# Local attention and a token/channel mixer in one kernel: q and k turned by transfer transposes into a permuted key layout, global query rows scored apart, part of the ReLUs on VectorE

## The chip, the cores and the metric

The kernel runs on one core of one Trainium2 chip. The metric is the device time of one execution in microseconds (us), the time of the slowest core, which here is the only one. A run more than 1.5% above the fastest of its kernel is marked slow. A time of the text is the median of all timed runs; a profile is one execution of them. A ratio is the mean time of one kernel's fast runs over that of the other's of the same rounds, so it is not quite the ratio of the two medians.

Names: PE is TensorE (matmuls), PEld its weight loads, ACT is ScalarE, DVE is VectorE, Pool is GpSimd, SP is SyncE. SP here only issues transfers, in program order.

## The reference

Eight batches, eight heads, 576 positions, head size 64. Attention with a window of 32 positions to each side and eight global positions (which see all and are seen by all), then a mixer: a token MLP (576 to 256 to 576) and a channel MLP (512 to 1536 to 512), each with a residual.

```python
scores = scale * q @ k.T                              # per batch and head
mask = (abs(i - j) <= 32) | is_global[i] | is_global[j]
x = softmax(where(mask, scores, -1e9)) @ v            # heads joined: (8, 576, 512)
h = relu(x.T @ w_tok1) @ w_tok2
u = x + h.T
out = u + relu(u @ w_ch1) @ w_ch2
```

## The kernel before

Per batch the kernel casts q and k to f16, turns them on PE so that the head dimension lies on the partitions (T), lets DVE copy the result out of PSUM (TE), scores five key tiles per pair of heads (S_), takes the exps on ACT and multiplies them by a band mask on DVE (SM). GK and OG handle the global rows and columns, PV multiplies by v, M1 and M2 are the token MLP, M3 turns u by four DMA transposes (uT), M4 is the up-projection (its PSUM tile is b1p) and M5 the down-projection (op). The scheduling is by hand: iteration b merges the "dense" list of batch b (M4, M5) with the "sparse" list of batch b+1 (everything from scores to uT) into one program order, by weights.

```python
def load_v16(b):                       # v of batch b, cast by the transfer, key order as in memory
    for c in range(NT):                # 5 transfers, issued by Pool
        nc.gpsimd.dma_start(out=vsh[b % 2][r0:r1, c, :, 0:D], in_=v[b, :, j0 : j0 + (r1 - r0), :]...)

def T(b, p):                           # 10 transposes on PE per pair of heads
    for ti, n in enumerate((qn, kn)):
        for t in range(NT):
            nc.tensor.transpose(out=pT[:, ti, P*t : P*t+P], in_=n[b % 2][:, t, 2*p : 2*p+2, :], identity=ident)

def TE(b, p):                          # four DVE copies out of PSUM, which also undo the order of the load
    nc.vector.tensor_copy(out=qT..., in_=pm)   # 128x512 f16
    ...

def S_(b, p, part):
    def score(ps, off, c):             # PSUM written without stride; 208 or 144 columns (16 of them global rows)
        for par in range(2):
            nc.tensor.matmul(ps[:, par, off : off + n], lhsT=kT[r, P*c : P*c+P], rhs=qf[r, lo : lo+n], ...)
    ...                                # then 3 exps per pair on ACT

def M3(b, part):                       # u turned by transfer
    nc.sync.dma_start_transpose(out=s["uT"][:, :, P*tau : P*tau+P], in_=s["u16"][:, tau, :])

def M4(b, j):
    ...                                # 4 matmuls into b1p
    nc.scalar.activation(out=s["b1"][:, j, :], in_=ps, func=AF.Relu)

# sparse(b), cut:
if b == 1:   u += [(5.0, lambda: None), gather_t(0), ..., t(0), t(1)]   # b1p of batch 0 go first
u += [sa(0), sb(0), t(2), t(3), ..., GK(b), OG(b), PV, M1, load_v16(n), M2, M3, T and TE of batch n]

# start: q,k of batch 0, then v of batch 0 (5 transfers), then q,k of batch 1, all on SP
```

The softmax here doesn't subtract the row's maximum and nothing guards it: scores larger than these inputs give would overflow.

## Time and profile before

| | before |
|---|---|
| time | 357.12 us median (354.12 to 358.76, 4 runs) |
| span of the profiled run | 352.9 us, mean granted PE clock 0.999 |
| first b1p of batch 0 (end of the "start") | 44.3 us |
| seven iterations | 42.6, 42.5, 37.2, 41.0, 36.7, 40.6, 37.1 us |
| tail | 31.0 us |

The table is read from the first b1p matmul of each batch in the timeline, and an iteration runs from one such matmul to the next. Odd iterations are longer because the last 64 rows of two batches are projected together there.

It leaves out the ReLUs: in the stretch that the prediction names, from 207.2 us to the last exp at 219.9, ACT is busy 10.70 of 12.70 us, and waits for b1p for the rest:

```profile
ACT b L611 <- PE b1p L608: 2.0, 3, 0.8
```

### The profile page before, as it was taken

How to read it: one execution, taken by the hardware profiler on the slowest of the kernel's cores; microseconds unless marked ns; L12 is line 12 of the kernel's file. 1: busy time of each engine (PE TensorE's matmuls, PEld its weight loads, DVE VectorE, ACT ScalarE, POOL GpSimd, SP SyncE). 2: the span in 40 equal slices, each digit the busy share in tenths (PEclk: the TensorE clock that was granted, in tenths of full speed). 3: DMA queues.
4: the chain of work that ended last, by engine and by line, in shares of the span. 5: the costliest groups of instructions: out<-in, count | busy, mean ns of one | idle time of the engine just before them, and what ended most of it. 6: DMA issues, size and time to landing. Idle time of an engine off the chain costs nothing.

```text
span 352.9 us, 6771 instructions
## 1 busy us (share of the span) xinstructions
PE 313.1 (89%) x2753; PEld 167.7 (48%) x2753; DVE 205.2 (58%) x450; ACT 172.1 (49%) x308; POOL 67.0 (19%) x106
## 2 busy tenths in 40 slices
PE   0567888897979999999999998999999998998994
PEld 0345444454446454554466453555465453543641
DVE  3998658647654468457654567547754567451021
ACT  2448358721866238650875239642864258212600
POOL 8988836220003000120003000220000000000000
PEclk9999999999999999999999999999999999999999
DMA  6999999595817558387919467485800430024012
GB/s 138 264 276 207 245 225 160 34 115 119 250 37 70 88 125 263 24 76 106 298 34 86 74 154 230 28 102 137 265 3 30 106 76 2 2 74 119 2 59 89
DMA packets 90046, 42.28 MB, mean 120 GB/s; under 512 B 64928, under 2 KB 85280, under 8 KB 90016
## 3 DMA queue, kind: packets, MB, share of 16 engines
q1 hardware_dynamic: 52528, 33.69, 35.9%
q0 software_dynamic: 37200, 8.16, 25.3%
q8 instruction: 21, 0.34, 0.4%
q14 instruction: 9, 0.07, 0.1%
q10 hardware_dynamic: 288, 0.01, 0.0%
HBM read 36.12 MB, written 9.44 MB: 129 GB/s over the span
## 4 chain that ended last, share of the span: by engine, by line
PE 60%; DVE 17%; ACT 13%; DMA 5%; issue 3%; SPq 1%; DVEq 0%; ACTq 0%
PE op L634 23%; PE b1p L608 11%; PE a1p L538 5%; PE hp L562 4%; ACT b L611 4%; DVE e_all L453 3%; ACT e_all L431 3%; PE pv L493 3%; PE pT L393 3%; DMA uT<-u 3%; PE b1lp L621 3%; PE pv L502 3%; ACT e_all L440 2%; PE pv L507 2%; DVE kT L405 2%
## 5 line engine op out<-in xcount | busy, mean ns | idle before, releaser
L608 PE MATMUL b1p<-uT,wc 128*128 128x512 f16 x384 | 94.9, 380 | 4.2 <-DMA uT<-u 4.1
L634 PE MATMUL op<-wc,b 128*128 128x512 f16 x384 | 90.8, 379 | 0.0
L611 ACT ACTIVATE b<-b1p 128x512 f16<-128x512 f32 x96 | 58.4, 625 | 46.1 <-PE b1p L608 45.5
L342 POOL DMA_DIRECT2D vsh<-in_v_dram x35 | 29.6, 850 | 153.8 <-PE pv L507 145.1
L431 ACT ACTIVATE e_all<-s 128x832 f16<-128x832 f32 x32 | 28.5, 892 | 57.1 <-issue 50.7
L634 PEld LDWEIGHTS <-b 128*128 128x128 f16 x384 | 36.2, 98 | 40.1
L608 PEld LDWEIGHTS <-wc 128*128 128x128 f16 x384 | 32.6, 97 | 40.8 <-issue 6.7
L638 DVE TENSOR_TENSOR osb<-u,op 128x512 f32<-128x512 f16 x32 | 22.0, 687 | 44.0 <-PE op L634 43.7
L453 DVE TENSOR_TENSOR e_all<-e_all,bandm 128x1040 f16<-128x1040 f16 x64 | 42.0, 697 | 1.2
L403 DVE COPY qT<-pT 128x512 f16<-128x512 f16 x32 | 22.0, 688 | 17.8 <-PE pT L393 15.7
L522 DVE RECIPROCAL rr<-pv 128x8 f32<-128x8 f32 (+1 forms) x40 | 8.3, 207 | 36.9 <-PE pv L507 28.1
L420 PE MATMUL s<-qT,kT 64*128 64x208 f16 (+1 forms) x320 | 24.7, 254 | 5.6 <-ACT e_all L443 2.3
L523 DVE TENSOR_TENSOR x<-pv,rr 128x512 f16<-128x512 f32 (+1 forms) x40 | 27.6, 691 | 1.4
L502 PE MATMUL pv<-vsh,e_all 128*128 128x66 f16 x320 | 28.3, 197 | 0.0
L502 PEld LDWEIGHTS <-e_all 128*128 128x128 f16 x320 | 24.6, 100 | 4.3 <-issue 2.6
L493 PE MATMUL pv<-rf,lf 128*128 128x264 f16 x80 | 21.6, 284 | 4.0 <-DVE rf L480 2.3
L507 PE MATMUL pv<-vsh,e_all 128*128 128x66 f16 x256 | 24.1, 197 | 0.0
L546 ACT ACTIVATE a<-a1p 128x1024 f16<-128x1024 f32 x7 | 7.2, 1024 | 34.5 <-PE a1p L538 27.4
L420 PEld LDWEIGHTS <-kT 64*128 64x128 f16 x320 | 11.3, 97 | 26.4 <-issue 20.6
L440 ACT ACTIVATE e_all<-s 128x576 f16<-128x576 f32 x32 | 21.9, 684 | 2.8 <-PE s L420 2.8
L567 DVE TENSOR_TENSOR u<-x,hp 128x1024 f16<-128x1024 f16 x14 | 16.9, 1220 | 10.3 <-PE hp L562 10.3
L393 PE MATMUL pT<-ident,qn 128*128 128x128 f16 x160 | 15.3, 230 | 8.1 <-ACT qn L354 4.3
(149 smaller groups left out, 394.6 us busy)
## 6 DMA issues: line engine op xcount, KB each, us to landing
out_dram<-osb SPq DMA_DIRECT2D x32, 256.0 KB, 2.2
lq<-in_q_dram SPq DMA_DIRECT2D x7, 1024.0 KB, 7.1
lk<-in_k_dram SPq DMA_DIRECT2D x7, 1024.0 KB, 8.8
wc<-in_moe_w_ch_dram POOLq DMA_DIRECT2D x6, 512.0 KB, 10.7
vsh<-in_v_dram POOLq DMA_DIRECT2D x21, 128.0 KB, 5.0
vsh<-in_v_dram POOLq DMA_DIRECT2D x14, 96.0 KB, 3.3
lq<-in_q_dram SPq DMA_DIRECT2D x4, 256.0 KB, 5.6
lk<-in_k_dram SPq DMA_DIRECT2D x4, 256.0 KB, 6.2
```

The lines of the kernel that those rows point to most:

```text
L342: nc.gpsimd.dma_start(out=vsh[b % 2][r0:r1, c, :, 0:D], in_=v[b, :, j0 : j0 + (r1 - r0), :].rearrange("h p d -> p h d"),)
L420: nc.tensor.matmul(ps[:, par, off : off + n], lhsT=kT[r, P * c : P * c + P], rhs=qf[r, lo : lo + n], start=True, stop=True,)
L431: nc.scalar.activation(out=e2[:, :, 1:3, 64:EW], in_=ps[:, :, 0 : 2 * W].rearrange("p h (c x) -> p h c x", c=2), func=AF.Exp, scale=scale)
L440: nc.scalar.activation(out=ends, in_=ps[:, :, 0 : 2 * QS].rearrange("p h (c x) -> p h c x", c=2), func=AF.Exp, scale=scale)
L453: nc.vector.tensor_mul(out=eh, in0=eh, in1=bandm)
L493: nc.tensor.matmul(ps[:, hf, 0 : NP * VW], lhsT=s["lf"][:, P * tau - sh : P * tau - sh + P], rhs=s["rf"][:, 2 * hf : 2 * hf + 2], start=b ...
L502: nc.tensor.matmul(o, lhsT=e_all[:, h, tau, EW - P - sh : EW - sh], rhs=vsh[b % 2][:, tau, h, :], start=b == 0 and hh == 0, stop=last and ...
L507: nc.tensor.matmul(o, lhsT=e_all[:, h, tau + 1, 0:P], rhs=vsh[b % 2][:, tau + 1, h, :], start=False, stop=last)
L523: nc.vector.tensor_tensor(out=x16s[b % 2][r, tau, :].rearrange("p (f h x) -> p f h x", f=2, h=NP), in0=pq[r, :, :, 0:D], in1=rr[r].unsquee ...
L608: nc.tensor.matmul(ps, lhsT=wc1[:, cc, P * j : P * j + P], rhs=s["uT"][:, cc, :], start=(cc == 0), stop=(cc == 3))
L611: nc.scalar.activation(out=s["b1"][:, j, :], in_=ps, func=AF.Relu)
L634: nc.tensor.matmul(ps, lhsT=w, rhs=wc2[:, j, :], start=(j == 0), stop=(j == NJ - 1))
```

## The change

The intent is to take work off PE, DVE and ACT. For batches 1 to 7, q and k are turned by DMA transposes out of f16 copies, so 40 PE transposes and their DVE copies per batch vanish. The load puts row 4p+i on partition p, and the transfer leaves keys ordered by i first. Keys are therefore left permuted inside each tile: v must be loaded in the same order, which takes 20 transfers in place of 5. Queries are put back in order by writing the scores into PSUM at a stride of four words. Global query rows leave the scores (192 columns for 208) and are scored apart in GK. Four of the twelve ReLUs per batch go to DVE.

The core of the diff, with cuts marked by dots:

```diff
 def load_v16(b):
-    for c in range(NT):                                     # 5 transfers
+    for rows, c, src in v_parts(b):                         # 20 transfers: 4 residues x 5 tiles
+        nc.gpsimd.dma_start(out=vsh[b % 2][rows, c, :, 0:D], in_=src)
...
+def turn_k(b, c):
+    src = xk[32 * c : 32 * c + 32] if c < NT - 1 else xr[0:32]
+    nc.sync.dma_start_transpose(out=kTs[b % 2][:, c]..., in_=src...)
+def turn_q(b, hp): ...                                      # 8 turns per batch, all on SP
...
 def score(ps, off, c):
-    ps[:, par, off : off + n], lhsT=kT[r, P * c : P * c + P], rhs=qf[r, lo : lo + n]
+    ps[:, par, off : off + n].rearrange("k (x i) -> k i x", i=4), lhsT=kT[r, c, p], rhs=qT[r, p, :, lo:hi]
...
 def GK(b):
+    for c in range(NT):
+        for p in range(NP):                                 # 20 matmuls of 16 columns
+            nc.tensor.matmul(gq[:, c, p], lhsT=kT[:, c, p], rhs=qgz[:, b, p], start=True, stop=True)
+    ...                                                     # then exp (ACT) and a multiply (DVE) into eg, which OG reads
...
+        if j % 2 and j < 8:
+            nc.vector.tensor_scalar(out=s["b1"][:, j, :], in0=ps, scalar1=0.0, scalar2=None, op0=ALU.max)
...
+def qk_pads1():
+    nc.gpsimd.memset(lr[0:32], 0.0)                         # lr takes the last rows of q and k
...
 # start, cut
+    qk_pads1()
     load_rest(1)
     load_qk(1, slice(0, H))
...
 # sparse(b): no dummy ahead of the scores of batch 1 any more; per batch n = b + 1
-    ..., T(n, 0), TE(n, 0), T(n, 1), TE(n, 1)
+    ..., turns of k and q between PV and M1, turn(tq[2]) as the last just ahead of load_v16(n), M2 and M3 (uT)
```

## The prediction

> **What bounds it now.** The page's busy table has PE at 313 of 352.9 us. The first b1p matmul of each batch stands in the timeline at 44.3, 86.8, 129.3, 166.5, 207.5, 244.3, 284.8 and 321.9: a 44 us start, seven iterations (37 us even, 41 us odd from the third on), a 31 us tail. In these iterations PE's gaps are small. With start-to-start times of the trace (512 columns 216 ns, 128-column transpose 56 ns) an even iteration has about 33.1 us of PE work in 36.75. The rest is lost mostly in the scores while ACT runs continuously (207.2 to 220.5, exps and ReLUs).
>
> **Removed per batch.** 40 PE transposes: 2.3 us of PE. Their DVE evictions (4 x (688+180+680+180) ns = 6.9 us) and four eg multiplies (1.0 us). Four of twelve 0.6 us ReLUs leave ACT for DVE (0.69 us each).
>
> **Added per batch.** Twenty 16-column matmuls for global rows: estimated 0.6 us PE, from the 30 ns spacing of the 66-column pv matmuls. They put a chain gk, exp, multiply, og on PE's path, about 1 us. Scores now write PSUM with a stride of four words. The Trainium skill's "PSUM — Partial Sum Buffer" (Specifications) says a non-contiguous pattern slows matmuls significantly; nothing in this trace shows it. At half rate scores cost 1.5 us more, mostly hidden behind ACT. Eight transfer transposes of 9.5 uT-sizes together: SP spends 1.25 us issuing one uT, so an estimated 11 us more of the in-order SP queue, while the engines need only about 0.6 us per uT. ACT gets 12 casts for 10. v takes 20 Pool issues for 5, with slack.
>
> **Steady state.** The ACT-bound part before the global scores shortens from 13.1 to about 11.2 us, so the up-projection phase gains 1.2 us, and transposes at the iteration's end give another 1.2. But the last q turn (about 2.1 us of SP) stands just ahead of the uT transposes in SP's order, and the PE work hiding them shrinks from about 8 to 6.7 us: I expect 2 to 2.7 us of waiting for uT per even iteration, 1 to 1.5 per odd one. Net: even about 36.3, odd 39.5. The first two gain more (42.6 and 42.5 to about 38 and 41).
>
> **Start.** v of batch 0 comes in 20 transfers behind SP's queue, so Pool's casts end near 24.5 rather than 20. Then Pool issues weights and gathers, and only then clears lr; the rest load of k for batch 1 waits for that clear, and the q and k loads behind it on SP. They move from 17 to about 39 us, landing near 50. ACT casts them before the first token ReLU, and scores of batch 1, which need the turns, stand before the first b1p. I expect that b1p at about 60, not 44.3: a loss of about 16 us, which eats the steady gain.
>
> **Sum.** 60+38+41+36.3+39.5+36.3+39.5+36+31 = 357.6 us in the profile, before 352.9; timed runs lie about 1% above. I say 357 us, range 345 to 371. Faster by over 2%: 0.22; within: 0.47; slower: 0.31.
>
> **Would show it.** First b1p near 60 with SP waiting on Pool (right). Waits of b1p for uT around 2 us each in even iterations. Score pairs of 192 columns spaced near 80 ns (no stride cost) or 160. DVE below 170 us busy.
>
> **Could be wrong.** Turns issuing faster or slower than uT by size; a larger stride cost; loads landing sooner; transfers contending so that uT lands late.

## More of the kernel before

The kernel before was run again beside every set of experiments, and its medians lie between 356.4 and 358.6 us.

From the page of the kernel before: the busy table, four rows of the table of 40 slices (busy tenths; PEclk is the granted clock in tenths), and two lines of the table of transfer queues (packets, MB, share of the 16 transfer engines).

```profile
PE 313.1 (89%) x2753; PEld 167.7 (48%) x2753; DVE 205.2 (58%) x450; ACT 172.1 (49%) x308; POOL 67.0 (19%) x106
PE   0567888897979999999999998999999998998994
PEclk9999999999999999999999999999999999999999
DMA  6999999595817558387919467485800430024012
q1 hardware_dynamic: 52528, 33.69, 35.9%
q0 software_dynamic: 37200, 8.16, 25.3%
```

PE is busy through nearly the whole span at full clock, and the transfer engines have slack from the second quarter on. The waits of PE (what it waited for: us in total, times, longest):

```profile
PE b1p L608 <- DMA uT<-u: 4.1, 4, 2.0
PE s L420 <- ACT e_all L443: 2.3, 6, 0.6
PE og L475 <- DVE eg L447: 1.2, 1, 1.2
```

These are small. The groups of instructions by shape (busy us, mean ns | idle before, and what ended it), for the scores on PE and for two of the three exps that read them:

```profile
L420 PE MATMUL s<-qT,kT 64*128 64x208 f16 x192 | 20.7, 267 | 0.8 <-DVE qT L381 0.3 <-DVE kT L409 0.3 <-ACT e_all L431 0.2
L420 PE MATMUL s<-qT,kT 64*128 64x144 f16 x128 | 10.1, 235 | 4.8 <-ACT e_all L443 2.3 <-DVE kT L409 1.3 <-ACT e_all L431 1.0
L431 ACT ACTIVATE e_all<-s 128x832 f16<-128x832 f32 x32 | 28.5, 892 | 57.1 <-issue 50.7 <-PE s L420 6.4
L440 ACT ACTIVATE e_all<-s 128x576 f16<-128x576 f32 x32 | 21.9, 684 | 2.8 <-PE s L420 2.8
```

The exps hardly wait for the scores (6.4 and 2.8 us in the whole run, most of it in the start). This is the reading on which the prediction called that phase bound by ACT.

## The result, and the profile after

The changed kernel took 407.94 us median (405.76 to 409.92, 4 runs) beside 357.12 us (354.12 to 358.76, 4 runs). The ratio of the fast runs is 1.1436, 95% interval 1.1349 to 1.1524: slower by 14%, far outside the predicted range. All outputs are right.

| | before | after | difference |
|---|---|---|---|
| first b1p | 44.27 | 74.69 | +30.4 |
| first iteration | 42.56 | 47.03 | +4.5 |
| next six iterations | 235.1 | 250.9 | +15.8 |
| tail | 31.0 | 31.4 | +0.4 |
| span | 352.9 | 404.0 | +51.1 |

The same parts of the page after:

```profile
PE 320.7 (79%) x2633; PEld 158.3 (39%) x2633; DVE 177.9 (44%) x350; ACT 167.2 (41%) x290; POOL 122.8 (30%) x206
PE   0576013778969999789969998989698999898995
PEclk9979556696998999999989999999989999999999
DMA  7859999991897449974997199929990373003112
q1 hardware_dynamic: 81673, 42.42, 49.6%
q0 software_dynamic: 42464, 8.18, 24.5%
```

DVE and ACT have less to do, as meant, but PE has more, with 120 instructions fewer. The row PE has a hole in the fifth to seventh slice (40 to 70 us), and the granted clock is about half there. Queue q1, which carries the turns, has 29,000 packets more. The waits of PE (hp is the second product of the token MLP, s the scores, og the product of the global rows), and the one of SP that stands behind the start:

```profile
PE hp L639 <- ACT a L604: 22.4, 1, 22.4
PE b1p L669 <- DMA uT<-u: 15.7, 6, 3.9
PE s L473 <- DMA qT<-xq: 8.6, 1, 8.6
PE og L536 <- DVE eg L524: 8.0, 7, 1.2
```

```profile
SPq L137 <- POOL qT L185: 16.2, 1, 16.2
```

Four things in five lines: a long wait in the start, uT late in six iterations, one wait for the first turns, and the chain of the global rows in each iteration. The scores and their exps by shape:

```profile
L473 PE MATMUL s<-qT,kT 64*128 64x192 f16 x256 | 33.7, 392 | 0.1
L473 PE MATMUL s<-qT,kT 64*128 64x128 f16 x64 | 9.5, 293 | 9.1 <-DMA qT<-xq 8.6 <-ACT e_all L490 0.5
L484 ACT ACTIVATE e_all<-s 128x256 f16<-128x256 f32 x32 | 12.3, 384 | 82.2 <-PE s L473 80.9 <-ACT b L675 0.8 <-ACT e_all L490 0.6
```

A matmul of 192 columns has 392 ns where one of 208 had 267. In start-to-start times of the trace, two matmuls of 192 columns (one per half of the array) take 162 ns; before, two of 208 took about 100. The 80.9 us of ACT need care: 68.7 us of it are ACT's pauses ahead of the first exp of batches 1 to 7 (8.2 to 10.7 us each), and the kernel before has that pause too (the 50.7 us under "issue"). Added up gap by gap in the trace, inside the score phases of batches 1 to 7 ACT waits 6.8 us for the scores, where it waited 0.5 before.

The start, from the chain that ended last (start us, us, what). First the kernel before, which has nothing but its own work there, then the changed kernel:

```profile
38.82 0.61 ACT a L543
43.64 0.59 ACT uT L588
44.27 1.89 PE b1p L608 x8
```

```profile
34.47 1.63 POOL wc L268 x2
36.10 1.81 POOL lr L184
37.91 0.26 POOL qT L185
38.82 15.69 DMA lk<-in_k_dram
54.53 2.18 ACT xk L395 x4
58.79 0.50 ACT a L604
62.04 11.55 DMA qT<-xq
74.76 1.82 PE b1p L669 x4
```

Pool clears lr only after its casts of v, the weights and the gathers; q and k of batch 1 stand behind that clear on SP (the view of SP's wait names qT L185, the instruction that follows the clear and starts as it ends); their landing takes 15.7 us; ACT casts them before the first token ReLU (a), for which PE waits 22.4 us; then the last turns of q take 11.6 us to land, and the scores that need them stand ahead of the first b1p. Two stages of the changed kernel by windows (start:end, length, busy times with counts, then granted clock, share of the transfer engines, GB/s):

```profile
50.00:60.00 10.00, 0.67 (x2) 0.25 (x2) 0.00 (x0) 4.75 (x9) 5.99 (x11) 0.50 1.29 133
80.00:90.00 10.00, 7.22 (x63) 3.36 (x62) 6.41 (x16) 5.56 (x10) 4.70 (x8) 1.00 1.25 140
```

PE's clock is halved while it stands idle, and it stays so for a while after: the b1p matmuls that start from 74.7 to 75.5 us are 402 to 427 ns apart, those of a group from 77.1 us on 216 to 226. The Trainium skill's "TensorE: Matmul & The Clock Gate" (Part 1) says that PE goes to half clock after an idle window of about 3.4 us; the trace agrees that a long idle stretch (22.4 us here) halves it. The runs give no sharp length: b1p ran at half rate after a wait of 2.2 us in e3, and at full rate after one of 3.3 us in e12.

The late uT, from the timeline of SP in the iteration that ends at 206.84 us (start us, us, what):

```profile
195.35 1.30 SPq L416 DMA_TRANSPOSE qT<-xq  x1
197.37 1.55 SPq L416 DMA_TRANSPOSE qT<-xq  x1
199.01 5.93 SPq L658 DMA_TRANSPOSE uT<-u  x4
```

and the queues between 200 and 204 us (packets, MB, share):

```profile
q0 software_dynamic: 1665, 0.18, 99.9%
q1 hardware_dynamic: 1612, 0.40, 81.1%
```

u was ready at about 197.8 us. Its four transposes stand behind a turn of q on SP, and they share the transfer engines with the v packets of the next batch (q0), which Pool issued from 191.6 to 201.3 us. Once v is through, q1 alone moved 1830 packets in the 2.5 us from 204.5, against 1612 in the 4 us before.

### The profile page after: what moved, and what is told of

The parts are those of the page before. It is cut to its first block, busy times and chain, and to the rows that moved or that the text cites. A ratio compares the mean times of both kernels' runs of the same rounds, so it can differ in the third digit from the quotient of the medians.

```text
span 404.0 us, 6676 instructions
## 1 busy us (share of the span) xinstructions
PE 320.7 (79%) x2633; PEld 158.3 (39%) x2633; DVE 177.9 (44%) x350; ACT 167.2 (41%) x290; POOL 122.8 (30%) x206
## 4 chain that ended last, share of the span: by engine, by line
PE 63%; DMA 15%; DVE 8%; SPq 5%; POOL 3%; issue 2%; ACT 2%; DVEq 0%; POOLq 0%
PE b1p L669 21%; PE op L698 18%; PE s L473 6%; DMA uT<-u 4%; DMA lk<-in_k_dram 4%; PE a1p L599 4%; PE hp L623 3%; SPq L658 3%; DMA qT<-xq 3%; DMA lv<-in_v_dram 2%; DVE x L584 2%; PE pv L554 2%; PE b1lp L685 2%; PE pv L563 2%; PE pv L568 2%
## 5 line engine op out<-in xcount | busy, mean ns | idle before, releaser
L383 POOL DMA_DIRECT2D vsh<-in_v_dram x140 | 84.1, 622 | 153.8 <-PE pv L568 114.8
L669 PE MATMUL b1p<-uT,wc 128*128 128x512 f16 x384 | 99.2, 398 | 15.7 <-DMA uT<-u 15.7
L675 ACT ACTIVATE b<-b1p 128x512 f16<-128x512 f32 x64 | 38.4, 600 | 62.6 <-PE b1p L669 46.0
L673 DVE TENSOR_SCALAR b<-b1p 128x512 f16<-128x512 f32 x32 | 22.1, 691 | 68.8 <-PE b1p L669 68.8
L490 ACT ACTIVATE e_all<-s 128x768 f16<-128x768 f32 x64 | 50.0, 809 | 2.9 <-PE s L473 2.7
L484 ACT ACTIVATE e_all<-s 128x256 f16<-128x256 f32 x32 | 12.3, 384 | 82.2 <-PE s L473 80.9
L473 PE MATMUL s<-qT,kT 64*128 64x192 f16 (+1 forms) x320 | 36.2, 373 | 9.2 <-DMA qT<-xq 8.6
L498 DVE TENSOR_TENSOR e_all<-e_all,bandm 128x960 f16<-128x960 f16 x64 | 38.8, 650 | 2.1 <-ACT e_all L490 2.0
L583 DVE RECIPROCAL rr<-pv 128x8 f32<-128x8 f32 (+1 forms) x40 | 8.2, 206 | 38.8 <-PE pv L568 37.3
L563 PEld LDWEIGHTS <-e_all 128*128 128x128 f16 x320 | 23.9, 98 | 2.5 <-issue 0.3
L639 PE MATMUL hp<-a,w 128*128 128x512 f16 x8 | 3.7, 584 | 22.4 <-ACT a L604 22.4
L395 ACT CAST xr<-lr 48x512 f16<-48x512 f32 x28 | 15.5, 612 | 13.9 <-DMA lr<-in_k_dram 13.9
```

Source lines behind the costliest of these rows:

```text
L383: nc.gpsimd.dma_start(out=vsh[b % 2][rows, c, :, 0:D], in_=src)
L473: nc.tensor.matmul(ps[:, par, off : off + n].rearrange("k (x i) -> k i x", i=4), lhsT=kT[r, c, p], rhs=qT[r, p, :, lo:hi], start=True, sto ...
L490: nc.scalar.activation(out=e2[:, :, c : c + 2, 64:EW], in_=ps[:, :, off : off + 2 * BW].rearrange("p h (c x) -> p h c x", c=2), func=AF.Ex ...
L498: nc.vector.tensor_mul(out=eh, in0=eh, in1=bandm)
L563: nc.tensor.matmul(o, lhsT=e_all[:, h, tau, EW - P - sh : EW - sh], rhs=vsh[b % 2][:, tau, h, :], start=b == 0 and hh == 0, stop=last and ...
L669: nc.tensor.matmul(ps, lhsT=wc1[:, cc, P * j : P * j + P], rhs=s["uT"][:, cc, :], start=(cc == 0), stop=(cc == 3))
```

## The experiments

Sixteen kernels were run. The columns before the time are read from the traces as above. Differences from the changed kernel are between runs of different sets, so small ones mean little.

| run | first b1p | 2nd iteration starts | next six | time | ratio to before |
|---|---|---|---|---|---|
| before | 44.3 | 86.8 | 235.1 | 356.4 to 358.6 | |
| after | 74.7 | 121.7 | 250.9 | 407.94 | 1.1436 |
| e1_early | 58.0 | 106.0 | 256.2 | 393.47 | 1.1036 |
| e2_srhs | 77.4 | 128.5 | 269.9 | 431.57 | 1.2115 |
| e3_vlate | 75.4 | 121.7 | 244.9 | 399.77 | 1.1227 |
| e4_brelu | 43.9 | 86.8 | 233.9 | 355.23 | 1.0001 |
| e5_contig | 76.1 | 122.6 | 245.9 | 401.59 | 1.1259 |
| e6_split | 74.3 | 122.2 | 250.4 | 410.84 (2 of 4 slow) | 1.1529 |
| e7_startdelay | 47.3 | 102.7 | 251.6 | 387.24 | 1.0871 |
| e8_tqlate | 75.5 | 121.3 | 247.4 | 401.91 | 1.1264 |
| e9_five | 47.4 | 100.1 | 230.0 | 360.40 | 1.0059 |
| e10_gate | 47.4 | 100.8 | 230.3 | 363.72 | 1.0161 |
| e11_hybrid | 47.1 | 95.9 | 231.9 | 361.40 | 1.0135 |
| e12_hybrid_strided | 49.7 | 94.4 | 238.2 | 368.10 | 1.0328 |
| e13_wc2first | 47.7 | 98.8 | 232.8 | 365.65 | 1.0230 |
| e14_gkgap | 46.3 | 99.3 | 227.1 | 359.40 | 1.0044 |
| e15_vfirst | 46.9 | 100.2 | 227.8 | 363.86 (1 of 6 slow) | 1.0194 |
| e16_five_gk | 47.1 | 97.0 | 225.8 | 355.58 | 0.9918 |

### e1_early: the clear of lr first on Pool

```diff
+nc.gpsimd.memset(lr[0:32], 0.0)      # at the top of Pool's order
 def qk_pads1():
-    nc.gpsimd.memset(lr[0:32], 0.0)
```

> After, with one line moved: the clear of lr stands first on Pool instead of behind the weights and gathers. Theory (the late start is the wait of batch 1's q and k loads for that clear): the loads leave at about 23 us instead of 38, the first b1p starts at 46 to 52 us instead of 74.7, time 380 to 388 us. Rival (the twenty v transfers and the weight traffic make it late): the loads leave early but the first b1p stays above 62 us, time above 394 us. The iterations after it keep their lengths.

Measured: 393.47 us (390.90 to 396.06), first b1p at 58.0. The clear explains 16.7 of the 30.4 us at the first b1p, and 14.5 us of the time; SP issues the loads of batch 1 at 22.5 to 23.9 us, where the last three of them left at 37.9 to 38.8. The rest lay elsewhere, so both theories were half right. The six later iterations were 5 us longer than in the changed kernel, though nothing in them was edited. In the trace most of that is longer waits for uT (18.4 us for 15.7 over the seven) and more b1p at half clock (28 for 13, a loss of 5.6 us for 2.5); e7, with the same clear, does not show it, and why uT came later in e1 stays open.

### e2_srhs: the stride in the operand, not in PSUM

```diff
-ps[...].rearrange("k (x i) -> k i x", i=4), ... rhs=qT[r, p, :, lo:hi]
+ps[...].rearrange("k (x i) -> k x i", i=4), ... rhs=qT[r, p, :, lo:hi].rearrange("k i x -> k x i")
```

> After, with the stride moved from the PSUM side of the score matmuls to the SBUF side (moving operand read with a stride, scores written without one). Theory (the strided PSUM write halves the rate): pairs of 192 columns are spaced 80 to 90 ns instead of 160, an iteration loses about 1.5 us, time 395 to 400 us. Rival (any stride on either side costs as much, or the permuted operand is slow for another reason): spacing 150 ns or more and time 404 us or more.

Measured: 431.57 us (430.13 to 432.11). PSUM is now written in order, and the pairs of 192 columns are 324 ns apart, twice the 162 of the changed kernel. Consecutive columns of the operand now lie 320 bytes apart in SBUF. The Trainium skill's "SBUF — State Buffer" (Specifications, Cachelines) gives lines of 16 bytes that need two or more hits for full bandwidth; this run agrees, and shows that the price is on reads for matmuls too. As a test of the PSUM stride the run is void, since it swaps one stride for a dearer one.

### e3_vlate: v held back until uT is used

```diff
 def load_v16(b):
+    if b > 2:   # tiny Pool copy that waits for b1 of batch b-2, so v cannot start beside the turns of u
+        nc.gpsimd.tensor_copy(out=vgate[:, b : b + 1], in_=st[b - 2]["b1"][:, 3, 0:1])
```

> After, with a tiny Pool copy that holds back the v loads of batches 3 to 7 until the next iteration's fourth b1p has been evicted, so that they no longer run beside the turns and the uT transposes. Theory (uT lands late since its packets share the engines with v's): the waits for uT in even iterations fall from 3 to 4 us to about 1, time 395 to 401 us. Rival (the last q turn ahead of uT in SP's order makes it late): waits for uT stay at 3 us or more, time 404 us or more.

Measured: 399.77 us (399.04 to 400.19), 8.2 us under the changed kernel. The same stretch of SP's timeline, where the four transposes of u had 5.93 us:

```profile
197.08 1.29 SPq L420 DMA_TRANSPOSE qT<-xq  x1
198.46 5.16 SPq L662 DMA_TRANSPOSE uT<-u  x4
```

PE's waits for uT fall from 15.7 to 9.9 us. The three long ones fall from 3.3 to 3.9 us to 1.6 to 3.2, and not to the 1 us expected. So the v loads beside uT are one cause, and not the only one. The Trainium skill's "DMA: Bandwidth & Descriptors" (Issuing engines are not separate DMA queues) says that transfers of all issuers "will ultimately run on the same 16 DMA engines and interleave with each other"; the run agrees (5.16 us of SP for 5.93, and 8.2 us of the time).

### e4_brelu: the ReLU split alone, in the kernel before

```diff
+if j % 2 and j < 8:
+    nc.vector.tensor_scalar(out=s["b1"][:, j, :], in0=ps, scalar1=0.0, scalar2=None, op0=ALU.max)
+else:
     nc.scalar.activation(out=s["b1"][:, j, :], in_=ps, func=AF.Relu)
```

> Before, with only the ReLU split of the change (j odd and below 8 on VectorE). If ScalarE bounds the score part of the up-projection phase in before, the score part shortens by 1 to 2 us an iteration, time 342 to 350 us. If PE or VectorE bounds it already, time within 1% of before.

Measured: 355.23 us (353.75 to 357.57) beside 356.37, ratio 1.0001, interval 0.9923 to 1.0079. Four of twelve ReLUs off ACT are worth nothing there. In its trace ACT waits 1.1 us for the scores in the same phase (206 to 218.5 us), where it had not waited for them before: what ACT no longer does, it spends waiting for PE. So ACT alone did not pace that phase.

### e5_contig and e6_split: PSUM without stride, and its control

To write PSUM in order, the exps must read it permuted, and a pattern over two tiles at once has too many dimensions. So e5 has one exp per key tile, 20 per batch for 12. e6 has the 20 exps and keeps the stride.

```diff
-ps[:, par, off : off + n].rearrange("k (x i) -> k i x", i=4)
+ps[:, par, off : off + n].rearrange("k (i x) -> k i x", i=4)        # e5 only
...
-nc.scalar.activation(out=e2[:, :, c : c + 2, 64:EW], in_=ps[two tiles], ...)
+for cc in range(2):                                                   # e5 and e6
+    nc.scalar.activation(out=o, in_=i_, ...)                          # e5: "k h (i x) -> k h x i" on the input
```

> The changed kernel, but scores are written to PSUM without stride (query order inside the tile permuted) and the exps read PSUM with the permuted pattern; that needs one exp per key tile, 20 per batch for 12. Theory (the four-word stride in PSUM halves the rate of the scores, and PE waits for nothing else there, so it is paid in full): pairs of 192 columns spaced 80 to 100 ns in place of 159, about 1.5 us of PE less per batch, 397 to 404 us, and at least 8 us under e6_split. Rival (the scores are hidden behind ACT, as predicted): no faster than e6_split, and both at or above 408.

> Control of e5_contig: the changed kernel with 20 exps per batch for 12 and nothing else; PSUM keeps its stride. If ACT has slack in the scores: 407 to 410 us. If ACT bounds them, 8 more instructions [...]are paid: 413 to 420 us.

Measured: e5 401.59 us (401.35 to 402.36), e6 410.84 us (405.73 to 412.49). Two of e6's four runs, 412.41 and 412.49, are slow; the fast ones, 405.73 and 409.27, lie in the range of the changed kernel, so these runs show no cost of the 20 exps by themselves. The pairs of 192 columns are 83 ns apart for 162, and the group shows it:

```profile
L473 PE MATMUL s<-qT,kT 64*128 64x192 f16 x256 | 21.9, 267 | 0.2 <-ACT e_all L497 0.2
```

The stride is paid: 5.8 us against the mean of the control's fast runs (at least 8 were expected), 6.3 against the changed kernel. It is less than 1.5 us in each iteration, and the trace shows where some went: the wait for uT grew (16.7 us, longest 4.7), and after four of the waits PE ran at half clock. In the six iterations, 26 b1p ran at half rate, which cost 5.1 us (their spacing beyond 216 ns, added up); in the changed kernel 13, which cost 2.5. A gain in one stage was partly given back at the next wait.

### e7_startdelay: some b1p ahead of the scores of batch 1

```diff
 # on top of e1_early, in sparse(b)
+if b == 1:
+    u += [(6.0, lambda: None)]
```

> e1_early (the clear of lr at the top) and in the first merged stage about half of the b1p stand before the scores of batch 1, which wait for the turns. Theory (the rest of the lost start is that b1p stands behind scores that wait for turns, while wc2 and v loads share the transfer engines): first b1p at 44 to 50 us in place of 58, whole time 382 to 388 us in place of 393. Rival (only the wait moves into the first iteration, since the turns land no earlier): first b1p at 44 to 50, but the first iteration longer by the same amount, whole time 390 to 396.

Measured: 387.24 us (386.60 to 390.03). The first b1p comes at 47.3 us, as before it came at 44.3, but the first iteration is 55.4 us long. Of 10.7 us at the first b1p, 6.2 remain in the time. Start and order of the start together are worth 20.7 us. The turns themselves still take long in this stage; SP needs 9.0 us for four turns of k in e1 (9.2 in e9), where a later iteration needs 5.2.

### e8_tqlate: the last turn of q behind uT

```diff
-u += turn(tq[2])
 ...M2, M3...
+u += turn(tq[2])
```

> The changed kernel, but the last turn of q of each batch is issued after the four transposes of u and not just ahead of them. Theory of the prediction (uT waits because a turn of 1.3 to 1.6 us stands ahead of it in the order of SP): waits of b1p for uT fall by 1.3 us each, 398 to 403 us. Rival (uT waits because the v loads and turns share the 16 transfer engines, as e3_vlate suggests): less than 3 us gained, 405 to 409.

Measured: 401.91 us (401.41 to 402.32), 6.0 us under the changed kernel; waits for uT 11.2 us for 15.7. So the order of SP is a second cause of the late uT. I had expected e3 and e8 to exclude each other; both hold.

### e9_five: all five repairs

The clear of lr, the delay, PSUM in order, v held back, the last q turn behind uT.

> The changed kernel with five repairs at once: the clear of lr at the top, half of the first b1p ahead of the scores of batch 1, scores contiguous in PSUM (20 exps per batch), v loads held back until b1 of an earlier batch is there, last q turn behind the turns of u. If the four causes are separate (start 20.7 us, PSUM 6.3, v 8.1, order of SP 6.0, all as measured singly): 366 to 368 us. If v and the order of SP are two sides of one wait (uT comes too late): 370 to 375 us. If something else of the 51 us is still unnamed, more.

Measured: 360.40 us (358.79 to 363.16), ratio 1.0059, interval 0.9982 to 1.0137. The single gains add up to 20.7 + 6.3 + 8.2 + 6.0 = 41.2 us; together they are worth 47.5. The waits of PE, and in the six later iterations no b1p at half clock:

```profile
PE og L545 <- DVE eg L533: 9.3, 7, 1.8
PE s L478 <- DMA qT<-xq: 6.3, 1, 6.3
PE b1p L678 <- DMA uT<-u: 4.6, 4, 1.4
```

The sum of the single gains was expected (366 to 368 us), so this expectation missed on the good side. The six later iterations now take 230.0 us, 5.1 fewer than before the change: about 37.1 and 39.6 us for even and odd ones, near the predicted 36.3 and 39.5. What remains is the start: the second iteration begins 13.2 us later than before.

### e10_gate: wc2 and v of batch 1 only after the turns

```diff
+nc.gpsimd.tensor_copy(out=tgate[:, 0:1], in_=qTs[1][:, NP - 1, 3, 0:1])
 load_wc2(0)
 load_v16(1)
```

> e9_five, and Pool issues the three wc2 loads and v of batch 1 only once the last q turn of batch 1 has landed (a one-column copy of it on Pool stands before them). Theory (in the start the turns crawl because 1 KB weight packets and v packets share the transfer engines with them): each turn of the start costs SP 1.2 to 1.6 us in place of 2 to 3.8, the last lands near 47 us in place of 56, the first iteration shortens from 55 to about 46 us, 7 to 9 us less than e9_five. Rival (the turns are slow by themselves, or wc2 then comes too late for the down-projection): the same as e9_five within 2 us, or slower.

Measured: 363.72 us (362.86 to 364.48), not faster: the median is 3 us above e9's, but the intervals of the two ratios overlap. The last turn was issued by 50.8 us in place of 54.6, but then PE waited 7.3 us for v. My theory of the start fell in its gain: PE's wait for the last q turn did shrink, from 6.3 us in e9 to 0.5, and the two q turns held SP for 4.7 us in place of 6.1 (the four of k, still beside wc1, for 9.0 us as in e9); but that only changed who is late.

### e11_hybrid and e12_hybrid_strided: batch 1 turned on PE; then with the stride again

```diff
 # e11, on top of e9
-    turn_k(1, ...), turn_q(1, ...)
+    T(1, p), TE(1, p) on PE and DVE, placed as in the kernel before    # batches 2 to 7 by transfer
 # e12: e11 with PSUM at stride four and 12 exps per batch
```

> e9_five, but batch 1 is turned on PE as batch 0 is (into the same permuted layout), so that only batches 2 to 7 use transfer transposes. e9_five stands 13 us behind the kernel before at the start of the second iteration (100.1 to 86.8) and gains 5 in the rest. Theory (that loss is the late landing of batch 1's turns): second iteration starts at 87 to 91 us, the later ones as in e9_five (37.0 even, 39.6 odd), 348 to 353 us: faster than the kernel before by 1 to 2.5%. Rival (the first stage is slow for another reason, such as the half clock after PE's idling or the 20 loads of v): second iteration at 96 or later, 356 or more.

> e11_hybrid with the scores again written to PSUM at the stride of four words, 12 exps per batch. It asks what the stride costs once uT no longer comes late. If the score phase is bound by PE there: about 1.5 us more per iteration, 9 to 13 us above e11_hybrid. If ACT bounds it, as the prediction said (stride mostly hidden, and 8 exps fewer): within 3 us of e11_hybrid.

Measured: e11 361.40 us (361.12 to 362.73), e12 368.10 us (365.85 to 370.70). e11 missed its range (348 to 353 us): the second iteration started at 95.9 us, not 87 to 91, for PE now waited for wc2, two of whose loads stood on Pool behind 20 issues of v. The pair answers its other question. From the third on, even iterations take 38.2 to 38.6 us with the stride and 37.1 to 37.3 without, odd ones 41.0 and 39.6, and the whole 6.7 us more. That is under the 9 to 13 us expected of a phase bound by PE and over the 3 us of one bound by ACT; the second iteration starts 1.5 us earlier with the stride, which takes a part back. ACT's waits for the scores of batch 5, first without, then with the stride:

```profile
ACT e_all L490 <- PE s L479: 10.5, 1, 10.5
ACT e_all L490 <- PE s L479: 12.3, 4, 10.7
```

The longest is the pause ahead of the phase; inside it the view lists no further wait without the stride, and three of 1.6 us in all with it. With uT no longer late after the second iteration, the stride is still paid, even though 8 exps per batch are saved with it.

### e13_wc2first, e14_gkgap, e15_vfirst, e16_five_gk: the start again, and the chain of the global rows

```diff
 # e13, on e11: order of issue on Pool
 load_wc2(0)
-load_v16(1)
 load_wc2(4)
 load_wc2(8)
+load_v16(1)
 # e14, on e13 (e16: the same edit on e9): one b1p falls between GK and OG in PE's order
-(0.3, lambda: GK(b)), (2.5, lambda: OG(b))
+(1.6, lambda: GK(b)), (2.5, lambda: OG(b))
 # e15, on e14: v of batch 1 before wc1(4), wc1(8) and wc2
```

> e11_hybrid, but Pool issues all three wc2 loads before the 20 loads of v of batch 1; in e11_hybrid two of them stood behind v, whose issue stalled, and PE waited for wc2 until 70 us. Theory (the v loads, 20 for 5, hold up what stands behind them on Pool): first iteration 42 to 44 us in place of 48.8, 353 to 357 us in all, about level with the kernel before. Rival (v of batch 1 then comes too late for its global scores): first iteration still 47 or more, 359 to 363.

> e13_wc2first with one b1p placed between the global scores and og (the order of PE alone; the weight of GK in the merge 0.3 to 1.6). Theory (the chain gk, exp, multiply, og that the change put on PE's path is open wait, 1.15 to 1.3 us per iteration): 0.8 to 1.1 us less in each of iterations 1 to 6, 6 to 8 us less than e13, about 346 to 350. Rival (the wait turns up elsewhere, ACT or uT): within 2 us of e13.

> e14_gkgap, but Pool issues v of batch 1 before the second and third block of wc1 and all of wc2 (after the gathers). In e11 and e13 the first iteration was 6 to 9 us longer than before, because Pool's 20 v issues alternate with large weight transfers: whichever of v and wc2 stands second comes late. Theory (it is the v loads waiting behind weights in one queue): v lands by 45 us, first iteration 42 to 45 us in place of 53, 346 to 351 us in all, 2 to 3% faster than before. Rival (all must pass the same engines, so the weights now come late instead): first iteration 48 or more, or the first b1p later by as much; 355 to 360.

> e9_five with the one b1p between the global scores and og. Theory (each iteration's gain of 1.0 to 1.3 us that e14_gkgap showed is independent of how batch 1 is turned): 353 to 356 us, 1 to 1.5% faster than before. Rival (the late uT or the start takes it back): 359 to 361, as e9_five.

Measured: e13 365.65 us (364.15 to 368.37), e14 359.40 (357.68 to 361.09), e15 363.86 (361.61 to 364.53 in its five fast runs), e16 355.58 (352.96 to 356.10). e13 and e15 came out above both ranges of their expectations, and e14 missed its absolute range while its gain over e13 was as expected. From the waits of PE in e13 and in e15:

```profile
PE og L546 <- DMA vsh<-in_v_dram: 4.6, 5, 3.5
```

```profile
PE s L479 <- POOL kT L187: 4.5, 1, 4.5
PE b1p L679 <- DMA wc<-in_moe_w_ch_dram: 3.1, 1, 3.1
```

With wc2 first, v is late; with v first, Pool's own clears and wc1 are late. No order of Pool that I tried brought the first iteration below 48.8 us without the stride (44.8 with it, where the first b1p came 2.6 us later). The gap between GK and OG was real and could be filled: e14 is 6.3 us under e13, and the third to the seventh iteration are each shorter by 1.1 to 1.3 us (the first two are longer). Its waits of og for eg, 8.0 us in seven iterations after the change, are down to:

```profile
PE og L546 <- DVE eg L534: 2.1, 4, 1.3
```

e16 is the best version: ratio 0.9918, interval 0.9867 to 0.9970. It beats both kernels, the one before by less than 1%.

## Why the prediction was wrong

The prediction said 357 us and found the right places. It failed by sizes, and in one place by reading a bound as a hiding place. Its sum, term by term, beside the profile of the changed kernel:

| | start | iterations 1 to 7 | tail | sum |
|---|---|---|---|---|
| predicted | 60 | 38, 41, 36.3, 39.5, 36.3, 39.5, 36 | 31 | 357.6 |
| measured | 74.7 | 47.0, 44.5, 40.6, 43.6, 41.2, 42.7, 38.3 | 31.4 | 404.0 |

Of the 46.4 us missed, 14.7 are the start, 9.0 the first iteration and 22.3 the six after it. With the stride, the order of v and the order of the last q turn repaired (e9), these six take 230.0 us where 228.6 were predicted, so points 2 to 4 together seem to hold nearly all of that part.

1. **The start: "I expect that b1p at about 60, not 44.3".** It came at 74.7. The mechanism was right (SP waited 16.2 us for Pool's clear, and the loads moved to 38 us, as written); e1 shows it is worth 16.7 us at that b1p. What failed is what comes behind it: the loads landed at 54.5 us for the expected 50, and the last q turns then took 11.6 us from issue to landing. The prediction named that path ("scores of batch 1, which need the turns, stand before the first b1p") and gave it no time; PE waited 8.6 us on it. It took SP's 1.25 us for a uT as the measure of a turn; here, with weights, gathers and v on 82% of the transfer engines (62 to 69 us), one q turn held SP for 5.5 us, and e10 shows PE's wait for it nearly gone with wc2 and v kept away. e7 shows that putting b1p ahead of the scores recovers another 6.2 us of time.

2. **The stride: "At half rate scores cost 1.5 us more, mostly hidden behind ACT".** The rate was right (162 ns per pair for 83). The hiding was the step that failed. "ACT runs continuously" was not so even before (10.70 of 12.70 us, with 2.0 us of waiting for b1p), and once PE writes the scores at half rate, ACT waits for them (inside the score phases of batches 1 to 7 6.8 us for 0.5 before, and 5.7 in e12 for 0.8 in e11). e11 and e12 put the price at 1.1 to 1.5 us per iteration from the third on, 6.7 us in all, with fewer exps on the side of the stride. A busy neighbour hides nothing if it is itself waiting for PE.

3. **uT: "2 to 2.7 us of waiting for uT per even iteration, 1 to 1.5 per odd one".** Over the seven iterations this forecast adds up to 11 to 15.3 us, and 15.7 were measured, so the term was nearly right in sum; the first three waits at the end of an even iteration were too long for it (3.3 to 3.9 us). The order on SP, which the prediction named, is worth 6.0 us (e8). What it missed is v: "v takes 20 Pool issues for 5, with slack". Pool has slack, but 20 issues of 0.6 us stretch v's packets over the stretch in which u is turned (e3: 8.2 us). The transfers were costed for who issues them, and not for whom they meet. "Transfers contending so that uT lands late" stood among the risks without a number.

4. **Half clock.** Not in the prediction. After some of the waits b1p ran at half rate: 13 in the six iterations, 2.5 us, and 10 in the first, 2.1 us. In the six iterations of the combined version (e9) there are none. This may be a part of why five repairs gave 6.3 us more than the sum of their single gains; I did not test it apart.

5. **Right.** The chain of the global rows, "about 1 us" per batch: 8.0 us in seven waits, and e14 gains 6.3 us by filling it. The tail: 31 us predicted, 31.4 measured. The steady state without the faults: e9 has 37.1 and 39.6 us for 36.3 and 39.5. Not right: DVE was to fall below 170 us and has 177.9.

6. **The ReLUs.** "The up-projection phase gains 1.2 us" from a shorter ACT-bound part found no support: in the kernel before, the split alone gains nothing (e4). It was not tested alone in the changed kernel.

What stays open: why the first iteration was 9.0 us longer than predicted, and why it remains at 49 to 53 us in the unstrided repaired versions, 6 to 11 us longer than before. The traces show only where PE stood: in e9 it waits in this iteration 6.3 us for qT, 2.4 for the gathered rows and 1.7 for eg, and its mean granted clock is 0.87 (0.90 in the changed kernel, 1.00 before). e10, e11, e13 and e15 moved the wait between qT, wc2, v and wc1, which fits a limit on what the start must move and issue as a whole. No run took away the 20 v issues, since the permuted key order needs them, so that cause is only argued.

## What to carry to other kernels

Ask of every transfer that a change adds not only who issues it and for how long, but which other transfer it will overlap and who waits for that one; two streams with slack on their own queues can still make the one that matters late. A cost "hidden behind" a busy engine is hidden only by as much as the other engine is ahead; look whether the busy engine is itself waiting in that phase, and compare the two rates before writing the cost off. When several small faults feed the same wait, single repairs can look weak (here 41.2 us one by one, 47.5 together); try them together before judging the idea.

## What the Trainium skill lacked or had wrong

- "PSUM — Partial Sum Buffer" (Specifications (TRN2)) says that a non-contiguous pattern slows matmuls significantly and gives no factor. Here a stride of four f32 words on the write doubled the spacing of a pair of 192-column matmuls, 162 ns for 83; for a pair of 128 columns it was only 78 for 66.
- "SBUF — State Buffer" (Specifications, Cachelines) gives no factor for a matmul operand either. A step of 320 bytes between columns made it 324 ns for the same pair (e2), dearer than the stride in PSUM.
- "DMA: Bandwidth & Descriptors" (Issuing engines are not separate DMA queues) says that the time to initiate a transfer is usually small relative to the transfer. For these transposes it is not small: a uT held SP for 1.25 us and landed 2.5 us after its issue (medians of the kernel before), and the four turns of k in the start, with weights and v on the transfer engines, held it for 9.2 us (e9).
- The same page gives no figure for what each piece of a split load costs the issuer: v in 20 transfers per batch held Pool 84.1 us in seven batches, in 5 transfers 29.6 us, for the same bytes.
